# Fillers, two transposes, a cast and several memsets of a fused attention and mixture kernel change place, under a new order

## Chip, cores, metric

One core of a Trainium2 chip runs the whole program. The metric is the device time of one execution in microseconds: 364.89 us as the median of 3 runs before the change (364.28 to 365.04).

## Reference, cut to what matters

```python
def reference(q, k, v, phi, w1, w2, w_in, w_out):
    # attention: B=4, H=8, S=576, D=64; heads 0-3 a window of 32, heads 4-7 of 128 with every 4th key
    scores = where(mask, q @ k.T / 8, -1e9)
    attn = softmax(scores) @ v
    x = attn.transpose(0, 2, 1, 3).reshape(2304, 512)
    # soft mixture: 8 experts with 4 slots each
    logits = x @ phi                               # 2304 x 32
    d = softmax over the tokens (axis 0)           # dispatch
    slot_input = (d.T @ x).reshape(8, 4, 512)
    slot_out = relu(slot_input @ w1[e]) @ w2[e]    # each expert e
    c = softmax over the slots (axis 1)            # combine
    x = c @ slot_out.reshape(32, 512)
    # dense layer
    h = x @ w_in                                   # 2304 x 2048
    return (h * sigmoid(h)) @ w_out                # 2304 x 512
```

## The kernel before, in words

**Stages.** Attention runs over 16 pairs of heads, four pairs to a batch. For pair n, SyncE loads q, k and v (`lq`, `lk`, `lv`), POOL spreads q into two halves of a buffer (`qx`, `qy`; for pair 0 `qy0` is VectorE's, line 178), TensorE makes the scores (`S`), VectorE the row maxima (`rm`), ScalarE the exponentials (`ex`), POOL normalizes (`nm`), VectorE transposes (`pt`), TensorE multiplies by v (`pv`), ScalarE copies (`xe`), TensorE transposes (`T`, line 312) and makes the logits (`lt`), and ScalarE stores x (`te`, line 315).

After each batch b comes its part of the dispatch softmax over the tokens, kept as a running maximum and a running sum: `da` (VectorE, maximum), `dt` (TensorE, transpose), `dm` (VectorE, line 381), `db` (TensorE, broadcast of the maximum), `dq` and `dr` (POOL and TensorE, the same maximum by rows), `dsub` (VectorE, line 397), `dex` (ScalarE, line 461), `dc` (TensorE, 40 matmuls with x), `dw`, `dwe`, `dacc` (rescaling), `ds` (VectorE, line 467: the sum in `acc`). Behind the last batch's `ds3`, `sit` transposes acc (TensorE, line 505), `sipz` (POOL) and `sipy` (VectorE) clear the padded buffer `x_sip`, and `sie` (VectorE, line 518) spreads the slots into it. `hzz` (POOL, line 514) clears the 2112 columns that `hr0` and `hr1` later fill.

The combine softmax runs beside it for each batch: `caa`, `cab`, `cac`, `cad`, `cae`, then `caf` (VectorE: a cast at line 417 and a subtraction at 418 into `cc`), `cag` (POOL, line 422), and `cb` (TensorE transposes, line 434; `cbB.0` has three, `cbB.1` has two), copied by `cbs`.

The experts are 16 steps `L1.i` (w1) and 16 steps `L2.i` (w2), each reading one weight of 128 x 2048 f32 (1,024 KB), with `he`, `ht`, `hr` (copy, transpose, relu) after each half of L1. `soe`, `sotm`, `sote` bring the slots' outputs back. In the dense layer `aq` multiplies them by w_in (so that 32 slots, not 2304 tokens, go through w_in), `ah` and `al` split the result into a high and a low part, `ac` lines them up; `h` multiplies by the combine weights, `si`, `gh`, `gl` make silu in two parts, `om` multiplies by w_out (three matmuls a step), `oe` evacuates. w_in and w_out arrive as 64-bit words, and VectorE converts each piece in three steps (lines 630, 632, 634: `cva`, `cvb`, `cvi` for w_in, `cvc`, `cvd`, `cvo` for w_out); `wh` and `wl` split w_out.

**Order.** Every step is put into a list with `op(name, engine, cost, deps, fn)`. `list_schedule` deals them out by a cost model: at each moment an engine takes its ready step with the longest remaining path plus `PRIO` of its kind. Each engine then runs its steps in that order. SyncE's loads have a fixed order: ten at the start, then the letters of `ATT` (q: q and k of the next pair, v: the next v, w: the next w1 or w2 weight, i and o: the first w_in and w_out parts), then the rest. A load waits for its buffer: w2.8 to w2.15 go where w1.0 to w1.7 or later were and wait for `L1.1` to `L1.8`; `lwi0.0` waits for `L1.11`, `lwo0` for `L1.14`. All loads before w_in's second piece (`lwi1.0`) are the same set in both kernels.

**Fillers.** `fl` and `ff` are bf16 matmuls of 512 columns whose results nobody reads. They read `cc`, the combine softmax's buffer, and run on TensorE at the start (`FILL`: how many ahead of pairs 0 to 3) and in the last dispatch softmax (`TAIL`: after which step, how many). L1.0 waits for all `ff`.

## Time and profile before

| what | us |
|---|---|
| median of 3 runs (lowest, highest) | 364.89 (364.28, 365.04) |
| the profiled execution | 362.87 |
| its span, first to last instruction | 361.1 |
| TensorE busy | 348.3 (96%) |
| VectorE busy | 236.9 (66%) |
| ScalarE busy | 165.0 (46%) |
| POOL busy | 74.2 (21%) |
| transfers | 70.02 MB, 194 GB/s over the span |

All times of rows are microseconds from the span's first instruction. The profiled execution is one run; its span leaves out 1.77 us around it. PE is TensorE, PEld its weight loads, DVE VectorE, ACT ScalarE, SPq SyncE's transfer queue. All TensorE helpers go through line 86, so there a row is told from the next by what it reads.

### The profile page before, as it was taken

How to read it: one execution, taken by the hardware profiler on the slowest of the kernel's cores; microseconds unless marked ns; L12 is line 12 of the kernel's file. 1: busy time of each engine (PE TensorE's matmuls, PEld its weight loads, DVE VectorE, ACT ScalarE, POOL GpSimd, SP SyncE). 2: the span in 40 equal slices, each digit the busy share in tenths (PEclk: the TensorE clock that was granted, in tenths of full speed). 3: DMA queues.
4: the chain of work that ended last, by engine and by line, in shares of the span. 5: the costliest groups of instructions: out<-in, count | busy, mean ns of one | idle time of the engine just before them, and what ended most of it. 6: DMA issues, size and time to landing. Idle time of an engine off the chain costs nothing.

```text
span 361.1 us, 7977 instructions
## 1 busy us (share of the span) xinstructions
PE 348.3 (96%) x3121; PEld 263.7 (73%) x3121; DVE 236.9 (66%) x547; ACT 165.0 (46%) x558; POOL 74.2 (21%) x121
## 2 busy tenths in 40 slices
PE   7999999999699999999999999999999999999995
PEld 3577778787423346778888888878788888888884
DVE  5778767799611559999999964479444744474445
ACT  1699998896140126595444342255452222222220
POOL 6779798575410000000000000000000000000000
PEclk9999999999999999999999999999999999999999
DMA  7999999999989999371830000000000300030004
GB/s 263 408 401 409 401 405 382 409 415 416 420 328 416 393 422 420 123 298 33 343 108 8 2 0 1 2 0 3 0 0 2 145 29 2 1 145 31 0 0 174
DMA packets 17460, 70.02 MB, mean 194 GB/s; under 512 B 1936, under 2 KB 2448, under 8 KB 11664
## 3 DMA queue, kind: packets, MB, share of 16 engines
q1 hardware_dynamic: 17424, 69.53, 49.1%
q8 instruction: 24, 0.39, 0.4%
q14 instruction: 12, 0.10, 0.1%
HBM read 64.80 MB, written 4.72 MB: 193 GB/s over the span
## 4 chain that ended last, share of the span: by engine, by line
PE 87%; DVE 6%; ACT 4%; issue 1%; POOL 0%; DVEq 0%; ACTq 0%
PE ps L86 83%; PE ps L312 3%; ACT rt_px L232 1%; ACT rv_astk L711 1%; DVE stats L227 1%; PE ps L434 1%; DVE ra_wif L634 1%; DVE ra_wif L632 1%; DVE chi L417 0%; ACT rt_gtm L794 0%; ACT x_gz L799 0%; POOL rt_px L249 0%; DVE w_gy L804 0%; DVE cc L418 0%; DVE ra_a L178 0%
## 5 line engine op out<-in xcount | busy, mean ns | idle before, releaser
L86 PE MATMUL ps<-w_ws,x_gz 128*128 128x512 f32 x432 | 107.5, 392 | 0.0
L794 ACT ACTIVATE rt_gtm<-ps 128x384 f32<-128x384 f32 x96 | 46.6, 492 | 103.4 <-PE ps L86 102.9
L86 PEld LDWEIGHTS ps<-w_ws,x_gz 128*128 128x128 f32 x432 | 80.1, 188 | 16.6 <-issue 0.4
L86 PE MATMUL ps<-w_ws,w_gy 128*128 128x512 f32 (+1 forms) x219 | 53.7, 389 | 0.0
L232 ACT ACTIVATE rt_px<-ps,spaced 128x64 f32<-128x64 f32 x144 | 43.7, 332 | 11.6 <-DVE spaced L228 10.8
L86 PEld LDWEIGHTS ps<-w_ws,w_gy 128*128 128x128 f32 x219 | 40.4, 188 | 8.1
L801 DVE CAST x_gz<-rt_gtm 128x384 fp32r<-128x384 f32 x52 | 18.6, 358 | 41.4 <-ACT rt_gtm L794 41.3
L804 DVE TENSOR_TENSOR x_gz<-rt_gtm,x_gz 128x384 fp32r<-128x384 f32 x64 | 35.5, 557 | 4.2
L86 PE MATMUL ps<-ct_ct,rv_astk 128*128 128x384 f32 x96 | 32.0, 340 | 0.2 <-ACT rv_astk L711 0.2
L232 ACT ACTIVATION_READ_ACCUMULATOR rt_px<-ps,spaced 128x1 f32 x144 | 32.1, 223 | 0.0
L801 DVE CAST w_gy<-rt_gtm 128x384 fp32r<-128x384 f32 x28 | 10.0, 357 | 20.2 <-ACT rt_gtm L794 20.1
L86 PEld LDWEIGHTS ps<-ct_ct,rv_astk 128*128 128x128 f32 x96 | 17.9, 188 | 5.3 <-ACT rv_astk L711 1.0
L249 POOL TENSOR_TENSOR rt_px<-rt_px,stats 128x576 f32<-128x576 f32 (+2 forms) x17 | 18.9, 1115 | 6.7 <-DVE stats L245 2.8
L804 DVE TENSOR_TENSOR w_gy<-rt_gtm,w_gy 128x384 fp32r<-128x384 f32 x32 | 17.8, 557 | 2.7 <-ACT rt_gtm L794 0.4
L86 PE MATMUL ps<-rk_ws,x_gz 128*128 128x512 f32 x72 | 18.0, 394 | 0.4 <-ACT x_gz L799 0.4
L86 PE MATMUL ps<-rb_ws,x_gz 128*128 128x512 f32 x72 | 18.0, 393 | 0.0
L86 PEld LDWEIGHTS ps<-rk_ws,x_gz 128*128 128x128 f32 x72 | 13.3, 188 | 3.3 <-ACT x_gz L799 0.7
L86 PEld LDWEIGHTS ps<-rb_ws,x_gz 128*128 128x128 f32 x72 | 13.3, 188 | 2.8 <-DVE rb_ws L755 0.2
L227 DVE TENSOR_REDUCE stats<-ps 128x9 f32<-128x576 f32 x16 | 11.8, 736 | 5.3 <-PE ps L86 3.3
L86 PE MATMUL ps<-cc 128*128 128x512 bf16 x37 | 11.0, 433 | 4.0 <-DVE cc L418 2.3
L86 PEld LDWEIGHTS ps<-rb_a,rv_v 128*64 128x64 f32 x320 | 13.1, 137 | 2.1 <-issue 1.1
L86 PE MATMUL ps<-rb_a,rv_v 128*64 128x96 f32 (+2 forms) x320 | 14.6, 241 | 0.0
(224 smaller groups left out, 520.1 us busy)
## 6 DMA issues: line engine op xcount, KB each, us to landing
w_wi<-in_w_in SPq DMA_DIRECT2D x7, 1024.0 KB, 12.8
w_wo<-in_w_out SPq DMA_DIRECT2D x5, 1024.0 KB, 6.9
rk_k<-in_k SPq DMA_DIRECT2D x12, 288.0 KB, 8.0
rs_raw<-in_v SPq DMA_DIRECT2D x9, 288.0 KB, 7.6
rs_raw<-in_q SPq DMA_DIRECT2D x8, 288.0 KB, 8.9
w_more<-in_q SPq DMA_DIRECT2D x8, 288.0 KB, 9.3
...
```

The costliest lines, as they stand in the source:

```text
L86: pe.matmul(out, lhsT=lhsT, rhs=rhs, start=start, stop=stop, skip_group_check=True)
L227: dve.tensor_reduce(out=mxs[:, n % 2], in_=ps[:, c:c + 64 * NJ].rearrange("p (j c) -> p j c", c=64), axis=AXX, op=ALU.max)
L232: act.activation(out=preg(n)[:, j, :], in_=sj(n, j), func=ACTF.Exp, scale=D ** -0.5, bias=nmx[:, r, j // 3, j % 3:j % 3 + 1], accum_out=su ...
L249: pool.tensor_tensor(out=p, in0=p, in1=rinv[:, n % 2, j0:j1].rearrange("p (j o) -> p j o", o=1).to_broadcast([128, j1 - j0, 64]), op=ALU.mult)
L312: pe.transpose(ps[0:m, c:c + 128], x[:, 128 * t:128 * t + m], ident)
L434: pe.transpose(cbank(b, k)[:, c:c + m], cc[0:m, t].rearrange("p r s -> p (r s)"), ident[0:m, 0:m])
L632: dve.scalar_tensor_tensor(out=out, in0=hi, scalar=0xC0000000, in1=out, op0=ALU.bitwise_and, op1=ALU.bitwise_or)
L634: dve.scalar_tensor_tensor(out=out, in0=lo, scalar=29, in1=out, op0=ALU.logical_shift_right, op1=ALU.bitwise_or)
L711: act.copy(out=asl(f)[32 * r:32 * r + 32], in_=(aqh if r < 2 else aql)[rows])
L794: act.activation(out=gtm(u), in_=hb(u), func=ACTF.Silu)
L801: dve.tensor_copy(ghalf(u, 0), gtm(u))
L804: dve.tensor_tensor(out=ghalf(u, 1), in0=gtm(u), in1=ghalf(u, 0), op=ALU.subtract)
```

## The change

The filler groups become three: two matmuls behind `dt3` (in bank 0 instead of 3), two behind `dr3`, one behind `cb1.1`; `dr3` also waits for the first. `caf1` waits for `dsub3`, `caf2` for `sie`, `cb1.1` for `dc3`, `cb1.0` for `sit`, `hzz` for `sie`. Of the start's VectorE memsets, `ilb`, `izb1` and `it1` wait for `qy0`. The first filler block has 8 matmuls instead of 7. The cost model lets the four engines start at 0.75 us and gives the first fillers 0.42 us each. `ATT` and all of `PRIO` are new.

```diff
@@ -455,7 +455,7 @@
            lambda b=b: mm(mb[:, 128:160], ones[0:1].to_broadcast([1, 128]), dm[:, 0:NS], True, True))
         op(f"dq{b}", "POOL", .28, [f"dm{b}", f"dr{pb}" if b else None], lambda b=b: pool.tensor_copy(
             dm[:, NS:].rearrange("p (r s) -> p r s", r=4), dm[:, 0:NS].rearrange("p (o s) -> p o s", o=1).to_broadcast([1, 4, NS])))
-        op(f"dr{b}", "PE", .3, [f"dq{b}", f"dsub{b}" if b < B - 1 else exn(NPAIR - 2), f"dw{pb}" if b else "ix"],
+        op(f"dr{b}", "PE", .3, [f"dq{b}", "ff0" if b == B - 1 else None, f"dsub{b}" if b < B - 1 else exn(NPAIR - 2), f"dw{pb}" if b else "ix"],
            lambda b=b: mm(drb(b), dm[:, NS:], ones[0:1], True, True))
         op(f"dsub{b}", "DVE", .27, [f"db{b}", f"la{b}", f"dc{pb}" if b else None], lambda b=b: dsub(b))
         op(f"dex{b}", "ACT", .24, [f"dsub{b}"], lambda b=b: act.activation(out=le, in_=le, func=ACTF.Exp))
@@ -475,12 +475,12 @@
         op(f"cac{b}", "ACT", .24, [f"cab{b}"], lambda b=b: act.activation(out=cn, in_=cn, func=ACTF.Exp))
         op(f"cad{b}", "DVE", .66, [f"cac{b}", f"cae{pb}" if b else None], lambda b=b: ca4(b))
         op(f"cae{b}", "POOL", .42, [f"cad{b}"], lambda b=b: pool.tensor_tensor(out=cn, in0=cn, in1=bc5(csm), op=ALU.mult))
-        op(f"caf{b}", "DVE", .68, [f"cae{b}"] + ([f"cb{pb}.0", f"cb{pb}.1"] if b else []), lambda b=b: ca6(b))
+        op(f"caf{b}", "DVE", .68, [f"cae{b}", "sie" if b == 2 else "dsub3" if b == 1 else None] + ([f"cb{pb}.0", f"cb{pb}.1"] if b else []), lambda b=b: ca6(b))
         op(f"cag{b}", "POOL", 1.2, [f"caf{b}"], lambda b=b: ca7(b))
         for k in range(2):
             e = exn(NPAIR - 1)
             free = (((e,), (e,)), ((f"xe{NPAIR-1}",), (e,)), ((f"xe{NPAIR-1}", f"te{NPAIR-1}"), (f"la{B-1}", f"da{B-1}")), (("cbs1.0",), ("he1",)))[b][k]
-            op(f"cb{b}.{k}", "PE", (.45, .3)[k], [f"cag{b}", *free], lambda b=b, k=k: cb(b, k))
+            op(f"cb{b}.{k}", "PE", (.45, .3)[k], [f"cag{b}", {"1.1": "dc3", "1.0": "sit"}.get(f"{b}.{k}"), *free], lambda b=b, k=k: cb(b, k))
             op(f"cbs{b}.{k}", "ACT", (.37, .21)[k], [f"cb{b}.{k}", "cbs0.0" if b or k else "L1.0"], lambda b=b, k=k: cbe(b, k))
 
 
@@ -511,7 +511,7 @@
 
     op("sipz", "POOL", .63, ["dc3"], lambda: pool.memset(sip(0, 704), 0.0))
     op("sipy", "DVE", .39, ["dc3"], lambda: dve.memset(sip(704, 352), 0.0))
-    op("hzz", "POOL", 1.8, ["sipz"], lambda: pool.memset(reg("sip", 1056, 2112), 0.0))
+    op("hzz", "POOL", 1.8, ["sie"], lambda: pool.memset(reg("sip", 1056, 2112), 0.0))
 
     def sie():
         dst = sipad().rearrange("p (e x) -> p e x", x=132)[:, :, 0:128].rearrange("p e (g i) -> p e g i", i=32)[:, :, :, 0:4]
@@ -919,25 +919,25 @@
         for _ in range(c):
             mm(bank[b], fsrc[:, 0:128], fsrc[:, 0:512], True, True)
 
-    for k, (d, c) in enumerate(TAIL):
-        op(f"ff{k}", "PE", .225 * c, [d, f"te{NPAIR-1}"], lambda c=c: fill(c, 3))
+    for k, (d, c, b) in enumerate(TAIL):
+        op(f"ff{k}", "PE", .225 * c, [d, f"te{NPAIR-1}" if b else exn(NPAIR - 1)], lambda b=b, c=c: fill(c, b))
         ops["L1.0"][2].append(f"ff{k}")
 
     def ilb():
         dve.memset(lb[64:128, 128:160], -1e30)
         dve.memset(ps[64:128, TC + 512:TC + 640], 0.0)
 
-    op("ilb", "DVE", .2, [], ilb)
+    op("ilb", "DVE", .2, ["qy0"], ilb)
     op("ifl", "DVE", .3, [], lambda: dve.memset(cc.rearrange("p t r s -> p (t r s)")[:, 0:256], 1.0))
     op("pex", "ACT", 1.6, ["ifl"], lambda: act.activation(out=t4[:, 7:8], in_=cc[:, 0, 0, 0:1], func=ACTF.Exp))
     for n in FILL:
-        op(f"fl{n}", "PE", .225 * FILL[n], ["ifl", f"S{n-1}" if n else None], lambda n=n: fill(FILL[n]))
+        op(f"fl{n}", "PE", (.225 if n else .42) * FILL[n], ["ifl", f"S{n-1}" if n else None], lambda n=n: fill(FILL[n]))
     for n in range(2):
         op(f"iza{n}", "POOL", .57, [], lambda n=n: pool.memset(zq(n, 1), 0.0))
-        op(f"izb{n}", "DVE", .57, [], lambda n=n: dve.memset(zq(n, 0), 0.0))
+        op(f"izb{n}", "DVE", .57, ["qy0"] if n else [], lambda n=n: dve.memset(zq(n, 0), 0.0))
     op("izm", "POOL", 2.7 + 1.3 * VY.count("POOL"), ["iza1", "qx0"], izm)
     for n in range(2):
-        op(f"it{n}", "DVE", .85, [], lambda n=n: dve.memset(ptreg(n), 0.0))
+        op(f"it{n}", "DVE", .85, ["qy0"] if n else [], lambda n=n: dve.memset(ptreg(n), 0.0))
     op("ix", "POOL", .7, ["izm"], ix)
     op("cmask", "SP", 1.2, [], cmask)
     op("cip", "SP", .37, [], lambda: sp.dma_start(out=ip, in_=a["ip"]))
@@ -993,7 +993,7 @@
         fixed = {"xe": (4, 5), "T": (3, 4), "te": (3, 4), "lt": (6,), "la": (6,), "da": (6,), "ht": (2,), "hr": (2,), "soe": (3,),
                  "aqh": (6,), "aq": (6,), "ah": (6,), "al": (6,), "aqr": (7,), "ahr": (7,), "alr": (7,)}
         fixed.update(dict.fromkeys(("dt", "dm", "db", "dsub", "dc", "ds", "sit", "sie", "fl"), (7,)))
-        fixed["ff"] = (3,)
+        fixed["ff"] = (TAIL[i[0]][2],) if kind == "ff" else ()
         if kind == "pv":
             return {4 if i[1] == (2 if i[0] == NPAIR - 1 else 1) else 5}
         return {3} if n.startswith("L2") else set(fixed.get(kind, ()))
@@ -1031,19 +1031,19 @@
 OMS = 1
 LOOK = 0.2
 AHEAD = 3.0
-ATT = "vqqwvvwqqwvqwwvvqwqvwqqvwvqwqvwvvwqwqwwvvwwwwwwwwwwwwwwiwoiwwowiw"
+ATT = "qqvqwvwwqvqwvvwqvvqwqwvqvqwvvqwwvqwwwqvwwwvwwwwwwwwwwwwwwooiwwwii"
 URG = {"al", "ac", "ah", "sote", "aqh", "sotm", "soe", "on", "aqr", "ahr", "alr", "aq", "h", "gh", "gl", "si"}
 SAME = {"DVE": .04, "ACT": .04, "PE": .0, "POOL": .02}
 LAT = {"SP": 2.85, "POOL": .05, "PE": .18, "ACT": .12, "DVE": .12}
 MORE = {"ex": .04, "xe": .1, "te": .1, "vy": .07, "rm": .06, "rc": .08, "da": .06, "la": .06, "dsub": .05, "dw": .05, "nm": .04, "dex": .1, "dwe": .1, "pt": .02}
 LATE = ((0, 0), (10, .8), (25, 1.6), (110, 2.4))
 TICK = 10.24 / 3
-TAIL = (("te15", 2), ("db3", 3), ("dc3", 2), ("sit", 2))
-FILL = {0: 7, 1: 6, 2: 6, 3: 9}
+TAIL = (("dt3", 2, 0), ("dr3", 2, 3), ("cb1.1", 1, 3))
+FILL = {0: 8, 1: 6, 2: 6, 3: 9}
 QP = range(1, 16)
 VY = ("DVE", "ACT", "DVE", "ACT")
 DUTY = {"dc": .5, "dt": .5, "db": .2, "dr": .0, "sit": .5, "ht": .28, "sotm": .28}
-PRIO = {'T': 0, 'nm': -3.27, 'om': -1, 'cae': -20, 'dacc': -0.36, 'pre': -0.5, 'dw': 0.5, 'da': -3.66, 'dsub': 1.06, 'soe': -4, 'rc': -0.5, 'wh': 1.11, 'dr': 0, 'dex': 4.35, 'cbs': 3, 'te': -5.49, 'dc': 2, 'he': -2, 'ah': -2.36, 'L': -1, 'S': -19.48, 'sie': -6, 'si': 0.16, 'pv': -0.65, 'cvd': 1, 'pt': -0.73, 'wl': 10, 'iq': -1, 'cad': 1.61, 'L2a': 0.5, 'cvi': 10, 'ex': -2.53, 'cvo': -4.15, 'aqr': 7.13, 'db': 4, 'ahr': -10, 'it': 10, 'gl': 3.48, 'gh': 10.52, 'dt': 0, 'ds': 6.4, 'la': -6, 'ng': 0.5, 'cac': -20, 'ht': -6, 'sote': 0.14, 'izm': -4, 'hzz': 4, 'sipy': 1, 'sit': -2.69, 'aq': 4, 'caf': 9.01, 'sipz': -7.48, 'al': 0.5, 'vy': -10.26, 'oe': 4, 'ac': 0.5, 'vx': -0.22, 'fz': 6, 'cab': -0.5, 'sotm': 10, 'alr': 0.01, 'cb': 4, 'lt': 2, 'cvb': -2.91, 'hr': 7.4, 'caa': 6, 'xe': 6.74, 'dwe': -3.34, 'on': -1.21, 'qx': -3, 'rm': -5.98, 'izq': -6.69, 'dm': -4, 'crs': 21.31, 'h': -0.95, 'cva': 0.96, 'cvc': -2.39, 'qy': -5.01, 'ix': -20.55, 'cag': 0, 'dq': -2.51, 'aqh': -4.57, 'fl': -2.55, 'ifl': 10, 'pex': 9.83, 'izb': -18.79, 'iza': -0.33, 'M': -1, 'ilb': 6, 'ff': 2}
+PRIO = {'T': 1.39, 'nm': 2, 'om': -2.0, 'cae': -2, 'dacc': 20, 'pre': -0.39, 'dw': 0.11, 'da': 20.17, 'dsub': 19.03, 'soe': -20, 'rc': 20.4, 'wh': 6.69, 'dr': 3, 'dex': 0.29, 'cbs': 1.51, 'te': -5.11, 'dc': -4, 'he': 10, 'ah': -4, 'L': -1, 'S': -1.43, 'sie': 6, 'si': -4.76, 'pv': 0.74, 'cvd': -4, 'pt': 1.57, 'wl': -4, 'iq': 10, 'cad': -1, 'L2a': -6, 'cvi': 2.11, 'ex': -3.75, 'cvo': -5.92, 'aqr': -3.34, 'db': 3.22, 'ahr': 0, 'it': -18.87, 'gl': -4, 'gh': -4.9, 'dt': -1.73, 'ds': 1.26, 'la': -0.47, 'ng': 0.5, 'cac': 9.13, 'ht': -3, 'sote': 5.24, 'izm': 0.31, 'hzz': -5.08, 'sipy': 10, 'sit': -6.08, 'aq': 10.56, 'caf': -1.65, 'sipz': -1.57, 'al': -6.1, 'vy': -9.58, 'oe': 4, 'ac': -4, 'vx': 1, 'fz': -10.07, 'cab': 20, 'sotm': -1, 'alr': -3, 'cb': -0.5, 'lt': 0.55, 'cvb': -4.67, 'hr': 1, 'caa': -7.65, 'xe': 2, 'dwe': -0.5, 'on': -1.51, 'qx': -4.09, 'rm': -1.72, 'izq': -6.69, 'dm': -4, 'crs': 1, 'h': -1.95, 'cva': -0.5, 'cvc': -6.64, 'qy': -3.36, 'ix': -1.65, 'cag': 1.87, 'dq': 9.0, 'aqh': -20, 'fl': 0, 'ifl': -0.41, 'pex': 0.18, 'izb': -4, 'iza': 3, 'M': 1.54, 'ilb': 0.32, 'ff': 3.95}
 
 
 def list_schedule(ops):
@@ -1080,9 +1080,9 @@
     for n in reversed(topo):
         level[n] = ops[n][1] + max((level[s] + gap(n, s) for s in succ[n]), default=0.0)
     idx = {n: i for i, n in enumerate(ops)}
-    free, ready = {}, {}
+    free, ready = dict.fromkeys(("PE", "ACT", "DVE", "POOL"), .75), {}
     when = dict.fromkeys(ops, 0.0)
-    events = [(0.0, idx[n], n) for n in ops if need[n] == 0]
+    events = [(0.0, idx[n], n) for n in ops if need[n] == 0] + [(.75, -1, None)]
     heapq.heapify(events)
     order = []
     work = {}
```

## Rows read from the trace of the kernel before

**Rows 1.** The page: share of the DMA engines in 40 slices of the span, in tenths.

```profile
DMA  7999999999989999371830000000000300030004
```

**Rows 2.** The chain of waits: start, us, what.

```profile
157.68 199.55 PE ps L86 x945
```

**Rows 3.** Timeline of VectorE, 99 to 160: start, us, what, idle before and its releaser.

```profile
133.35 0.76 DVE L630 TENSOR_SCALAR w_wif<-w_wi 128x512 uint32<-128x512 uint32 x2 [0.28 <-DMA w_wi<-in_w_in]
...
151.18 0.69 DVE L634 SCALAR_TENSOR_TENSOR ra_wif<-w_wi,ra_wif 128x512 uint32<-128x512 uint32 x1
```

**Rows 4.** Stretch, length, busy PE PEld DVE ACT POOL, granted clock, DMA share, GB/s.

```profile
133.35:151.87 18.52, 18.08 (x161) 14.11 (x162) 17.08 (x35) 10.28 (x28) 0.00 (x0) 1.00 0.72 298
```

**Rows 5.** The same view, around the start of L1.

```profile
98.00:100.00 2.00, 0.85 (x6) 0.27 (x10) 1.42 (x4) 0.00 (x0) 0.58 (x2) 1.00 1.00 418
100.00:102.00 2.00, 2.00 (x24) 0.65 (x20) 0.00 (x0) 1.18 (x5) 0.69 (x2) 1.00 0.63 262
102.00:104.00 2.00, 2.00 (x24) 0.52 (x16) 0.68 (x3) 1.84 (x4) 0.46 (x1) 1.00 0.73 164
```

**Rows 6.** Timeline of SyncE, 99 to 160: the load of w2.8.

```profile
101.67 0.33 SPq L534 DMA_DIRECT2D w_w2.8_1693<-in_w  x1
```

**Rows 7.** Timeline of TensorE, 84 to 101.

```profile
92.27 0.59 PE L86 MATMUL ps<-cc 128*128 128x512 bf16 x2 [0.47 <-ACT x_xb L315]
92.79 0.40 PE L86 MATMUL ps<-hsb,ones 1*128 1x32 f32 x2
...
93.98 0.47 PE L434 MATMUL ps<-ip,cc 128*128 128x128 f32 x2
94.38 1.45 PE L86 MATMUL ps<-x_xb,le 128*32 128x129 f32 x40
...
96.20 0.49 PE L434 MATMUL ps<-ip,cc 128*128 128x128 f32 x3
96.53 0.27 PE L505 MATMUL ps<-ip,acc 128*128 128x128 f32 x1
99.15 0.61 PE L86 MATMUL ps<-cc 128*128 128x512 bf16 x2 [2.35 <-DVE cc L418]
99.69 1.06 PE L86 MATMUL ps<-ct_w1.0_243,x_sip 128*32 128x512 f32 x8
```

**Rows 8.** Timeline of VectorE, 84 to 101.

```profile
84.17 0.21 DVE L417 CAST chi<-cn 128x160 fp32r<-128x160 f32 x1
...
91.83 0.28 DVE L381 TENSOR_REDUCE hsb<-ps 1x32 f32<-1x128 f32 x1 [0.38 <-PE ps L86]
...
95.90 0.35 DVE L467 SCALAR_TENSOR_TENSOR acc<-ps,wgt,acc 128x129 f32<-128x129 f32 x1 [0.69 <-PE ps L86]
...
96.76 1.74 DVE L417 CAST chi<-cn 128x160 fp32r<-128x160 f32 x1
...
99.01 0.28 DVE L518 COPY x_sip<-ps 128x128 f32<-128x128 f32 x1
```

**Rows 9.** Timeline of POOL, 84 to 101: the large memset.

```profile
96.55 1.86 POOL L514 MEMSET x_sip<- 128x2112 f32 x1
```

**Rows 10.** Timeline of ScalarE, 84 to 101: the last dispatch exponential.

```profile
93.58 0.34 ACT L461 ACTIVATE le<-le 128x160 f32<-128x160 f32 x1 [0.34 <-DVE le L397]
```

**Rows 11.** Timeline of VectorE, 0 to 14: the spread of pair 0's q.

```profile
4.65 0.95 DVE L178 TENSOR_SCALAR ra_a<-rs_raw 64x576 f32<-64x576 f32 x1
```

**Rows 12.** Timeline of POOL, 0 to 14: its copy of the same load.

```profile
3.68 0.66 POOL L180 COPY ra_a<-rs_raw 64x576 f32<-64x576 f32 x1 [1.86 <-DMA rs_raw<-in_q]
```

**Rows 13.** Timeline of TensorE, 0 to 14: first fillers, S0, S1.

```profile
1.19 3.17 PE L86 MATMUL ps<-cc 128*128 128x512 bf16 x7 [1.19 <-DVE cc L931]
5.70 2.19 PE L86 MATMUL ps<-rk_k,ra_a 128*64 128x64 f32 x36 [1.35 <-DVE ra_a L178]
...
10.37 1.27 PE L86 MATMUL ps<-rk_k,rb_a 128*64 128x64 f32 x36
```

**Rows 14.** Busy time by engine, summed over 13.26 to 91.4 us.

```profile
sum 78.14, PE 76.41 PEld 60.05 DVE 62.33 ACT 66.16 POOL 59.77; mean PE 12.73 PEld 10.01 DVE 10.39 ACT 11.03 POOL 9.96
```

## Prediction

> **What bounds the kernel now.** I read three views in this order: the 40 slices of the page for the transfers, the chain of waits for the end, then the timelines of the stretches that the change touches.
>
> The slices [rows 1] show two regimes. The DMA row stands at 9 from the second slice to the sixteenth (9 to about 144 us), with one 8 in the twelfth slice (99 to 108 us); behind it the queue is nearly empty. The chain of waits [rows 2] ends in one piece of TensorE work without a gap, 945 matmuls from 157.68 to 357.24 us. So the time is the moment at which TensorE reaches 157.68 in a state from which it never waits again, plus a tail that the change leaves alone. Anything saved earlier counts only as far as it moves that moment.
>
> What sets it? On VectorE the w_in conversion that starts at 133.35 waits for its load [rows 3], the first 1,024 KB w_in piece behind the last w2 weights. From there to the conversion that ends at 151.87 (the input of aq3) VectorE is busy 17.08 of 18.52 us [rows 3, 4]. aq3, its low parts, their copies on ScalarE and the matmul at 157.68 follow. So the moment hangs on a landing, and the landing on how long the transfers sat idle. They did so once: at 418 GB/s before 100 us, then 262 and 164 GB/s in two stretches of 2 us [rows 5]. Lost: (418-262)x2 + (418-164)x2 = 820 KB, or 820/418 = 1.96 us. The reason is in SyncE's row: the load of w2.8 is issued at 101.67 [rows 6], because its buffer is the one that L1.1 has just read, and L1.0 starts only at 99.69 [rows 7].
>
> **Why L1.0 starts so late.** The last dispatch softmax is a serial ping-pong, and TensorE waits 2.35 us ahead of 99.15 [rows 7]. VectorE shows why [rows 8]: the spread copy sie, which L1 needs, stands at 99.01 behind caf2. That cast took 1.74 us from 96.76, where another of its shape took 0.21 us; POOL's 2112-column memset ran from 96.55 to 98.41 [rows 9], and the cast ended 0.09 us after it.
>
> **The change, part by part.**
>
> (a) Cast and large memset behind sie. The transpose sit ends at 96.80. The two small memsets that sie also needs stand ahead of the cast on VectorE and ahead of the large memset on POOL, so they are done by 96.76. So sie may run at 96.92 instead of 99.01: -2.09 us. Both now follow sie. Nothing on the path waits for the cast (its transposes are cb2, in the experts' second half) or the memset (hr0, behind the first half of L1), so I cost them at nothing; without that cover the cast costs up to 1.74-0.21 = 1.5 us.
>
> (b) Fillers. The two between te15 and db3 go: db3 runs at 92.79, while its input, the maximum at 91.83, is done at 92.11 [rows 7, 8]. The new ff0 sits in the wait for that maximum (two matmuls, 0.59 us, from about 91.8), so db3 may start at about 92.35: -0.45. The three behind db3 become two behind dr3 and still fit beside VectorE and ScalarE. The two just ahead of L1.0 (99.15 to 99.69) go; L1.0 then starts some 0.1 us after sie's end (99.29) instead of 0.4: -0.3.
>
> (c) Transposes cb1.1 and cb1.0. Today cb1.1 runs at 93.98, and dc3 starts at 94.38 though its exponential ended at 93.92 [rows 7, 10]: -0.33. Moved behind dc3, cb1.1 (0.47) and one filler (0.3) may hold sit back: without them it starts after ds3, 0.35 us at 95.90, so they have a hole of 0.45 us to lie in and cost 0 to 0.3. cb1.0 (0.49) now follows sit instead of preceding it and lies beside sie: -0.2 to 0. I take 0 for the pair. caf1 now waits for dsub3; VectorE has 0.69 us idle and more before ds3, so 0.7 us of caf1 fits if the low-urgency sums behind it yield; queued behind it are dw3 and the rescaling of acc, for which ds3 waits. Between 0 and +0.5; I take 0.
>
> Sum of (a) to (c): 2.09 + 0.45 + 0.3 + 0.33 = 3.2 us earlier for L1.0.
>
> (d) Start. qy0 starts at 4.65 behind memsets [rows 11], while POOL's copy of the same load starts at 3.68, when it lands [rows 12]. With it1, izb1 and ilb moved behind qy0, it can start at 3.68 and end at 4.63. The first filler block grows from 7 to 8; seven took 3.17 us from 1.19 [rows 13], so eight end at about 4.8, and S0 moves from 5.70 to 4.8: -0.9. S0 takes 2.19 us against 1.27 for S1's equal matmuls at 10.37; without the idle 1.35 us ahead of it it may shorten by up to 0.92, at worst not at all. I take 0, so -0.9 (bounds -1.8 and 0). The moved memsets land in VectorE's idle time behind qy0, while S0 runs.
>
> The Trainium skill bears on (a) and (d). SBUF — State Buffer, section "Who interferes with whom", says that VectorE's cast and plain tensor_scalar can share a port pair with GpSimd, and that whoever issues first holds it for the whole instruction. The 1.74 us cast agrees. By that rule qy0, released together with POOL's 0.66 us copy, may wait for it: (d) would be -0.3 instead of -0.9, rival 1 below would give 0.6 us more, and the forecast would stay, since it doesn't use the whole of (d). The row of qy0 (0.95 us, beside POOL memsets) suggests that such a wait is already in it.
>
> (e) New order. All priorities and the order of the loads change, so attention (13.3 to 91.4 us) is dealt anew. TensorE is busy 76.41 of 78.14 us there [rows 14]: at most 1.73 us to gain. A loss has no bound in a row; the longest single wait ahead of TensorE is the 2.35 us in rows 7, so I allow +2.4. Value: 0, since no row favours a sign. In the loads, two more w2 weights come ahead of w_in and w_out, whose first parts come in one group with the last w2. The bytes ahead of the 133.35 load are the same. SyncE now waits for L1.14 ahead of w2.14; w2.8 to w2.13, 6 x 1,024 KB or 15 us at 418 GB/s, lie ahead of that wait, more than the 13 us from L1.1 to L1.14, so the queue shouldn't run dry.
>
> **Sum.** L1.0 moves by -3.2 - 0.9 = -4.1 us, to about 95.6 (bounds 93 to 99). To close the transfer gap w2.8 must be issued 2 us earlier; -4.1 does it with 2.1 to spare. From there all loads land 1.96 us earlier, and no more, because the queue is then full throughout. VectorE starts the w_in conversions at 131.4 and the moment 157.68 becomes 155.7. The other 2.1 us turn into TensorE waiting for w2.14, w2.15 and aq's converted weights. So -2.0 us. The profiled execution of 362.87 us (span 361.1, 1.77 around it) would become 360.9; the median of the runs, 364.89, is 2.02 above that execution, and with the same difference the forecast is **362.9**. Its own range is 362.1 to 364.1 (gains of 0.8 to 2.8: L1.0 only 1 us earlier, or VectorE's 1.4 idle us partly used).
>
> **Rivals.**
>
> 1. The landing doesn't bind. If the new order keeps TensorE fed while the w_in conversions are late, the end moves by the whole 3.2 to 4.1: 360.8 to 361.7, about 361. For it: between 136.38 and 157.68 TensorE waits little, so matmuls might be shifted. Against it: 17.08 of 18.52 us of VectorE between landing and aq3. Chance 0.15.
>
> 2. Nothing comes through. Attention lasts over 2 us longer, so the transfer gap stays, or the saved 2 us are lost in the conversions: 364.9. Chance 0.15.
>
> 3. Slower: VectorE's order from the landing to aq3. There the low parts of the activations (gl), which TensorE needs next, compete with the conversions, and gl's priority falls from 3.48 to -4, wl's from 10 to -4, while cvb and cvc fall less. Each conversion step put ahead of a gl or wl on the path costs 0.69 us [rows 3]. It decides from the third such step on (2.0/0.69 = 2.9); five give +1.5: 366.4. For it: VectorE has no slack there. Against it: the conversions' priorities fall too, and a step ahead of gl isn't lost but done early. Chance 0.20.
>
> **Chances.** Forecast 0.50, rivals 0.15, 0.15 and 0.20. Measurement can tell about 0.2%, or 0.73 us, from no change. Faster: 0.50 + 0.15 = 0.65. Within: 0.15. Slower: 0.20. The range goes from 360.4 (rival 1 with part of S0's shortening) to 366.2 (short of rival 3's far half): about 0.13 is left out.
>
> **What would show it.** Right: sie directly behind sit, and L1.0 at 94 to 97.5; the cast still long but with nobody waiting; S0 near 4.8; transfers at 410 GB/s or more from 100 to 104; w2.8 issued before 100; the first w_in conversion that waits for its load near 131.4; the last gap of TensorE ending near 155.7. Wrong: L1.0 later than 97.7 (attention lost time), a gap in the transfers at another place, such as 105 to 115 behind SyncE's wait for L1.14, or a first aq that waits for the late w_in parts so long that TensorE's last gap moves less than the landing.

## The result, and the profile after

The changed kernel takes **359.85 us** (median of 4 runs, 359.53 to 360.57); four runs of the kernel before in the same comparison gave 364.58 (362.69 to 365.04). The ratio is 0.9883, 95% interval 0.9844 to 0.9921. A second measurement of both (e6_after below) gave 0.9892 [0.9857, 0.9927]. The forecast was 362.9 us and the range began at 360.4: the direction was right, but the gain of 4.7 us is more than twice the 2.0 that was forecast, and the time lies below the range.

The two profiled executions are much closer together: 362.87 us before and 360.57 us after, -2.30. So there are two things to find: what the 2.3 us are, and why the medians differ by twice as much.

The slices of the page (share of the DMA engines, in tenths) have no dip left at the twelfth slice, where [rows 1] has an 8; and in the chain of waits (start, us, what) TensorE's last piece without a wait begins at 154.78 instead of 157.68 [rows 2] (the chain splits it at 169.06 over 0.01 us):

```profile
DMA  7999999999999999462630000000000400040004
```

```profile
154.78 14.26 PE ps L86 x63
169.06 185.50 PE ps L86 x882
```

TensorE's timeline in the tail of the last dispatch softmax (start, us, instruction, idle time before and its releaser), against [rows 7]:

```profile
92.43 0.38 PE L86 MATMUL ps<-ip,gmx 128*1 128x128 f32 x2
92.75 0.60 PE L86 MATMUL ps<-cc 128*128 128x512 bf16 x2
93.28 0.40 PE L86 MATMUL ps<-hsb,ones 1*128 1x32 f32 x2
...
94.46 1.45 PE L86 MATMUL ps<-x_xb,le 128*32 128x129 f32 x40
95.84 0.53 PE L434 MATMUL ps<-ip,cc 128*128 128x128 f32 x2
96.31 0.39 PE L86 MATMUL ps<-cc 128*128 128x512 bf16 x1
96.64 0.33 PE L505 MATMUL ps<-ip,acc 128*128 128x128 f32 x1
96.81 0.49 PE L434 MATMUL ps<-ip,cc 128*128 128x128 f32 x3
97.42 1.06 PE L86 MATMUL ps<-ct_w1.0_283,x_sip 128*32 128x512 f32 x8
```

The 2.35 us wait is gone. L1.0 starts at 97.42 instead of 99.69, and everything from dt3 (92.43) to L1.0 takes 4.99 us. In the kernel before dt3 stood at

```profile
91.42 0.38 PE L86 MATMUL ps<-ip,gmx 128*1 128x128 f32 x2
```

so the same stretch took 8.27 us. VectorE shows why (same columns, the changed kernel), with POOL's large memset in the second fence:

```profile
97.08 0.29 DVE L518 COPY x_sip<-ps 128x128 f32<-128x128 f32 x1
...
97.92 1.07 DVE L413 TENSOR_SCALAR csm<-csm 128x5 f32<-128x5 f32 x1
...
99.85 0.24 DVE L417 CAST chi<-cn 128x160 fp32r<-128x160 f32 x1 [0.44 <-POOL cn L477]
```

```profile
97.11 1.86 POOL L514 MEMSET x_sip<- 128x2112 f32 x1
```

sie (L518) now stands 0.11 us behind sit's end. The memset now meets another VectorE instruction, the 128x5 one of L413, and it is that one that ends 0.02 us behind the memset. The cast, ahead of sie before, comes 2.8 us after it and takes 0.24 us.

The start (TensorE, VectorE, POOL, same columns), the load of w2.8, and the w_in conversion that waited for its load before, with VectorE's step ahead of it, against [rows 13], [rows 11], [rows 12], [rows 6] and [rows 3]:

```profile
4.82 1.27 PE L86 MATMUL ps<-rk_k,ra_a 128*64 128x64 f32 x36 [0.22 <-POOL zm L901]
...
9.02 1.27 PE L86 MATMUL ps<-rk_k,rb_a 128*64 128x64 f32 x36 [0.61 <-POOL rb_a L180]
```

```profile
3.79 0.46 DVE L178 TENSOR_SCALAR ra_a<-rs_raw 64x576 f32<-64x576 f32 x1 [0.95 <-DMA rs_raw<-in_q]
```

```profile
3.82 0.95 POOL L180 COPY ra_a<-rs_raw 64x576 f32<-64x576 f32 x1 [2.00 <-DMA rs_raw<-in_q]
```

```profile
99.41 0.33 SPq L534 DMA_DIRECT2D w_w2.8_1683<-in_w  x1
```

```profile
130.61 0.43 DVE L634 SCALAR_TENSOR_TENSOR w_wif<-w_wi,w_wif 128x256 uint32<-128x256 uint32 x1
131.14 0.77 DVE L630 TENSOR_SCALAR w_wif<-w_wi 128x512 uint32<-128x512 uint32 x2
```

The transfers around the start of L1 (stretch, length, busy times of the engines, granted clock, DMA share, GB/s), against [rows 5]:

```profile
98.00:100.00 2.00, 2.00 (x24) 0.53 (x18) 1.53 (x4) 1.31 (x4) 1.42 (x2) 1.00 1.00 418
100.00:102.00 2.00, 2.00 (x24) 0.65 (x20) 0.77 (x3) 0.54 (x2) 1.19 (x2) 1.00 0.91 332
102.00:104.00 2.00, 2.00 (x24) 0.63 (x20) 0.50 (x3) 1.29 (x2) 0.45 (x1) 1.00 1.04 426
```

Of the 1.96 us of lost transfer time (418-332)x2/418 = 0.41 us are left. The conversion starts at 131.14 instead of 133.35, -2.21. It no longer waits: VectorE's step ahead of it ends at 131.04, so the row tells only that the load had landed by then.

Two more places on TensorE decide between the explanations below. The expert step L2.8 waited 0.38 us for `hr1` (line 548) before, and doesn't wait now (first fence: before, then after). The first `aq`, 64 matmuls, stands behind L2.15 and the slots' outputs (second fence, the same two kernels):

```profile
123.82 1.07 PE L86 MATMUL ps<-w_w2.8_1693,x_sip 128*32 128x512 f32 x8 [0.38 <-DVE x_sip L548]
120.99 1.06 PE L86 MATMUL ps<-w_w2.8_1683,x_sip 128*32 128x512 f32 x8
```

```profile
133.47 1.95 PE L86 MATMUL ps<-w_wif,lg 128*32 128x128 f32 x64
130.64 1.95 PE L86 MATMUL ps<-w_wif,lg 128*32 128x128 f32 x64
```

The times of the kernel before are best understood with the mean granted clock of each execution beside them. In the comparisons below it ran 76 times: 49 executions had a mean of 0.997 or more (median 362.69 us, 361.80 to 364.58), 27 had 0.993 to 0.995 (median 364.65, 363.56 to 365.21); the median of all 76 is 363.14. What spreads the 49 over 2.8 us isn't shown. All ten executions of the changed kernel had 0.998 or more (median 360.2).

### The profile page after: what moved, and what is told of

The parts are those of the page before. It is cut to its first block, busy times and chain, and to the rows that moved or that the text cites. A ratio compares the mean times of both kernels' runs of the same rounds, so it can differ in the third digit from the quotient of the medians.

```text
span 358.4 us, 7976 instructions
## 1 busy us (share of the span) xinstructions
PE 346.7 (97%) x3118; PEld 263.2 (73%) x3118; DVE 236.9 (66%) x547; ACT 165.1 (46%) x558; POOL 74.5 (21%) x121
## 4 chain that ended last, share of the span: by engine, by line
PE 90%; ACT 3%; DVE 2%; POOL 1%; issue 1%; DMA 1%; DVEq 0%; ACTq 0%; POOLq 0%
PE ps L86 86%; PE ps L312 3%; ACT rt_px L232 1%; DMA rs_raw<-in_q 1%; PE ps L434 1%; POOL rv_v L907 1%; ACT rv_astk L711 1%; ACT rt_px L301 1%; ACT rt_gtm L794 0%; POOL rb_a L180 0%; ACT x_gz L799 0%; POOL ra_a L180 0%; DVE stats L227 0%; ACT x_xb L315 0%; DVE spaced L244 0%
## 5 line engine op out<-in xcount | busy, mean ns | idle before, releaser
L86 PEld LDWEIGHTS ps<-ra_a,rv_v 128*64 128x64 f32 x320 | 13.3, 137 | 3.2 <-issue 1.4
L86 PE MATMUL ps<-ra_a,rv_v 128*64 128x96 f32 (+2 forms) x320 | 15.1, 241 | 0.6 <-issue 0.3
```

Of the source, the lines that this page charges most:

```text
L86: pe.matmul(out, lhsT=lhsT, rhs=rhs, start=start, stop=stop, skip_group_check=True)
```

## The experiments

In all of them "the tail" is the stretch from dt3 to L1.0. "L2.15" is how long the last w2 step takes (about 1.06 us without a wait). "Conversion" stands for the start of the w_in conversion that in the kernel before waits for its load; its wait for that load stands in brackets. "First aq" is the start of the 64 matmuls shown above, and "last gap" the start of TensorE's last piece without a wait (in e8_mix the start of the same step). This table gives the marks of each profiled execution, in us, and the comparison of all runs.

| kernel | L1.0 | w2.8 issued | L2.15 | conversion (wait) | first aq | last gap | first aq to gap | this execution | median (n) | ratio, 95% |
|---|---|---|---|---|---|---|---|---|---|---|
| before | 99.69 | 101.67 | 1.06 | 133.35 (0.28) | 133.47 | 157.68 | 24.21 | 362.87 |  |  |
| after | 97.42 | 99.41 | 1.04 | 131.14 (none) | 130.64 | 154.78 | 24.14 | 360.57 | 359.85 (4) | 0.9883 [0.9844, 0.9921] |
| e0_before | 99.20 | 101.19 | 1.47 | 133.32 (0.73) | 133.38 | 157.57 | 24.19 | 362.75 | 362.89 (12) | 0.9983 [0.996, 1.0005] |
| e1_start | 99.20 | 101.18 | 1.85 | 133.69 (1.10) | 133.75 | 157.99 | 24.24 | 363.14 | 363.46 (12) | 0.9986 [0.9962, 1.0009] |
| e2_tail | 96.81 | 98.80 | 1.55 | 130.99 (0.79) | 131.07 | 155.28 | 24.21 | 360.43 | 360.78 (7) | 0.9922 [0.9893, 0.9951] |
| e3_both | 95.35 | 97.34 | 2.98 | 131.16 (2.06) | 131.23 | 155.41 | 24.18 | 360.65 | 360.69 (6) | 0.9908 [0.988, 0.9935] |
| e4_bridge | 98.37 | 100.36 | 1.07 | 131.87 (none) | 132.16 | 156.33 | 24.17 | 361.50 | 362.11 (12) | 0.9959 [0.9935, 0.9983] |
| e5_nofill | 99.19 | 102.80 | 1.69 | 135.14 (0.95) | 135.21 | 159.41 | 24.20 | 364.66 | 363.07 (12) | 0.9985 [0.9958, 1.0011] |
| e6_after | 97.33 | 99.32 | 1.92 | 132.65 (1.05) | 131.41 | 156.09 | 24.68 | 361.78 | 360.29 (6) | 0.9892 [0.9857, 0.9927] |
| e7_short | 95.03 | 97.01 | 1.06 | 129.62 (0.80) | 129.06 | 153.25 | 24.19 | 358.43 | 358.69 (6) | 0.9848 [0.9816, 0.9881] |
| e8_mix | 95.45 | 97.44 | 2.21 | 131.10 (1.07) | 129.82 | 154.87 | 25.05 | 365.60 | 366.16 (6) | 1.0088 [1.0056, 1.012] |
| e9_hzz | 97.46 | 99.45 | 1.36 | 131.47 (0.62) | 131.53 | 155.72 | 24.19 | 360.93 | 361.47 (12) | 0.9953 [0.9936, 0.9971] |
| e10_before | 100.40 | 103.52 | 1.53 | 135.70 (0.80) | 135.76 | 159.95 | 24.19 | 365.16 | (1) |  |
| e11_start | 98.54 | 101.46 | 1.62 | 133.72 (0.88) | 133.78 | 157.99 | 24.21 | 363.15 | (1) |  |

### e0_before, e1_start, e2_tail, e3_both: the start and the tail, each alone and together

e0_before is the kernel before, unchanged. e1_start takes the start alone: one filler more ahead of S0, and VectorE's order there (the names are those of the kernel).

```diff
-VectorE: ifl it0 it1 iq0 iq1 iq2 iq3 ilb iq4 izb0 izb1 qy0
+VectorE: iq0 ifl iq1 iq2 izb0 iq3 iq4 it0 qy0 izb1 ilb it1
-fl0: 7 fillers
+fl0: 8 fillers
```

e2_tail takes the tail alone, with the order of the changed kernel on four engines; e3_both has both edits. Everything else, the order in attention and in the conversions too, is that of the kernel before.

```diff
-TensorE: dt3 ff0 db3 dr3 ff1 cb1.1 dc3 ff2 cb1.0 sit ff3 L1.0
+TensorE: dt3 ff0 db3 dr3 ff1 dc3 cb1.1 ff2 sit cb1.0 L1.0
-POOL: cag1 dq3 cab2 cae2 sipz hzz cag2 cab3
+POOL: dq3 cag1 sipz cab2 hzz cae2 cag2 cab3
-VectorE: ... ds3 sipy fz caf2 sie caa3 ...
+VectorE: ... caf1 dacc3 sipy ds3 fz sie cad2 caa3 caf2 ...
```

> The kernel before, unchanged, so that its own executions can be laid side by side. If executions of one program agree, every span lies within 0.3% (1.1 us) of 361.1 and the new trace has its steps where the first one had them: S0 at 5.70 for 2.19 us, L1.0 at 99.69, the last gap of TensorE ending at 157.68. If the first trace was a fast one among slower ones, the median is 363 to 365 and the new trace shows in which stretch 1 to 2 us are lost.

> The kernel before with the start alone: it1, izb1 and ilb behind qy0, 8 fillers instead of 7; order of everything else and all loads as before. S0 near 4.8. Landing theory (the end follows the landing of the w_in piece, which moves by no more than L1.0 does and no more than 2.0 us): L1.0 0.9 to 1.8 us earlier and the end 0.9 to 1.8 us earlier. TensorE theory (the end follows L1.0 all the way): the same 0.9 to 1.8 us. New-order theory (the start is absorbed in attention and the gain of the change comes from its priorities): 0 to 0.3 us.

> The kernel before with the tail alone: fillers, cb1.0, cb1.1, caf1, caf2 and hzz where the changed kernel has them, start, attention and loads as before. Both theories: L1.0 about 3.2 us earlier. Landing theory: the end 1.6 to 2.2 us earlier, because the loads had only 2.0 us of idle time to give back. TensorE theory: 3.0 to 3.4 us earlier. New-order theory: under 1 us.

> The kernel before with start and tail as in the changed kernel, but its own priorities and load order. L1.0 4.1 to 5 us earlier. Landing theory: the end no more than 2.2 us earlier, as in the tail alone. TensorE theory: 4.1 to 5 us earlier. New-order theory: clearly less than the changed kernel's 4.3 us, and the rest is the order's.

Measured: e0_before's twelve executions run from 362.16 to 364.58, two of them with the lower clock. In its profiled one L1.0 is 0.49 us earlier than in the first profile and the last gap only 0.11, because L2.15 takes 1.47 us instead of 1.06.

The start alone is no measurable gain (0.9986, interval across 1), where 0.9 to 1.8 us were expected if it comes through. S0 starts at 4.75 and S1 at 8.94 instead of 10.31, but in this execution the lead of 1.4 us shrinks through the pairs of attention and L1.0 starts at 99.20, as in e0_before. The tail alone gives 0.9922, most of the whole. With both, L1.0 starts 1.46 us earlier than with the tail alone, and the end gains nothing: 360.69 against 360.78. Against the full-clock executions of the kernel before in this comparison (median 362.69) each of the two gains 2.0 us, inside the 1.6 to 2.2 expected if the transfers bind; if TensorE's own work did, e3_both would have gained 4.1 to 5. The reason is in e3_both's timelines of TensorE and VectorE and in its transfers:

```profile
128.70 1.05 PE L86 MATMUL ps<-w_w2.15_1826,x_sip 128*32 128x512 f32 x4 [0.88 <-DMA w_w2.15_1826<-in_w]
```

```profile
131.16 0.76 DVE L630 TENSOR_SCALAR w_wif<-w_wi 128x512 uint32<-128x512 uint32 x2 [2.06 <-DMA w_wi<-in_w_in]
132.68 0.29 DVE L707 TENSOR_TENSOR rv_astk<-ps,rv_astk 64x128 fp32r<-64x128 f32 x1 [0.76 <-ACT rv_astk L704]
```

```profile
98.00:100.00 2.00, 2.00 (x24) 0.60 (x20) 0.77 (x3) 0.60 (x2) 1.19 (x2) 1.00 1.02 426
100.00:102.00 2.00, 2.00 (x24) 0.65 (x20) 0.43 (x3) 1.22 (x2) 0.46 (x1) 1.00 1.02 418
```

No transfer time is lost any more, and two steps wait for loads: L2.15 on TensorE for the second half of w2.15, and VectorE 2.06 us for the w_in piece, the load right behind it. VectorE's wait costs nothing, because its next step (L707) waits 0.76 us more for ScalarE's copy of the first aq's product, and the first aq stands behind L2.15. The chain of waits goes the same way: from the load of w2.15 at 117.29 to L2.15, and on through TensorE. So from L1.0 at about 97 on the transfers bind, as the prediction said, and rival 1 falls here (rival 2, nothing comes through, falls with e2_tail); but the load that binds is not the one that the prediction named.

### e4_bridge and e9_hzz: the 2.35 us wait alone

e4_bridge keeps every order of the kernel before and replaces the two fillers ahead of L1.0, which wait for the cast's product, by nine that read the mask, which is there from the start, so TensorE is busy through the wait. e9_hzz moves one instruction: POOL's large memset, behind the copy cag2.

```diff
-ff3: 2 fillers, operand cc
+ff3: 9 fillers, operand maskid
```

```diff
-POOL: sipz hzz cag2 cab3
+POOL: sipz cag2 hzz cab3
```

> The kernel before in its own order; only the two fillers ahead of L1.0 are replaced by nine that read the mask buffer instead of cc and so don't wait for caf2: they fill TensorE's 2.35 us wait behind sit. L1.0 doesn't come earlier (0 to 0.5 us). Clock theory (executions of the kernel before differ because the granted clock falls in some of them around that wait): the executions with a mean granted clock of 0.993 to 0.995 vanish, the spread of 361.9 to 365.1 shrinks to under 1.2 us, and the median falls from 363.5 to 362.2 to 362.8. Landing theory alone: no change of the median (within 0.4 us) and the same spread.

> The kernel before in its own order; only the 2112-column memset is put behind cag2 in POOL's queue, so that it no longer runs beside caf2's cast. If the memset held the cast back, the cast takes 0.2 to 0.3 us instead of 1.74 and L1.0 comes 1.3 to 1.6 us earlier; landing theory: the end 1.0 to 1.6 us earlier in executions at the full clock, and clock theory: TensorE's wait of 2.35 us shrinks to 0.8 to 1.0, so executions at 0.993 to 0.995 vanish and the median falls by 1.8 to 2.6 us. If the cast is slow for another reason, nothing changes.

Measured: e4_bridge 0.9959, e9_hzz 0.9953, and in both all 12 executions have a mean granted clock of 0.998 or more. In e9_hzz VectorE and TensorE read:

```profile
96.05 0.22 DVE L417 CAST chi<-cn 128x160 fp32r<-128x160 f32 x1
...
96.79 0.28 DVE L518 COPY x_sip<-ps 128x128 f32<-128x128 f32 x1
```

```profile
96.93 0.60 PE L86 MATMUL ps<-cc 128*128 128x512 bf16 x2 [0.84 <-DVE cc L418]
97.46 1.07 PE L86 MATMUL ps<-ct_w1.0_243,x_sip 128*32 128x512 f32 x8
```

The same cast in the same place takes 0.22 us once the memset isn't beside it (1.74 in [rows 8]). That one move brings sie to 96.79, cuts the wait from 2.35 to 0.84 us and carries 1.85 us to the last gap (155.72, against 157.57 in e0_before).

Both also show how much is the clock. Against the full-clock executions of the kernel before in the same comparisons (medians 362.38 and 362.61) e4_bridge gains 0.3 us and e9_hzz 1.1; the rest of the 1.5 us that each gains on the median is the lower group, which no longer occurs. For e9_hzz 1.8 to 2.6 us had been expected. e4_bridge doesn't part clock and order cleanly: its L1.0 came 0.83 us earlier than in e0_before, where 0 to 0.5 was expected.

### e5_nofill, e10_before, e11_start: where the clock falls

e5_nofill is the kernel before without the nine fillers of the tail. e10_before and e11_start are e0_before and e1_start once more, each for a single execution.

```diff
-ff0 ff1 ff2 ff3: 2, 3, 2, 2 fillers
+ff0 ff1 ff2 ff3: none
```

> The kernel before in its own order without the nine fillers of the last dispatch softmax. Clock theory: the mean granted clock is at or below 0.995 in every or nearly every execution, and the time is 364 to 366, at or above the slow half of the kernel before; its trace shows the stretch of the lower clock. Landing theory alone: L1.0 0.3 to 0.7 us earlier and the end the same or 0.5 us earlier.

> The kernel before again, for a look at an execution with a lower mean clock: of 76 executions of it 27 had a mean granted clock of 0.995 or less (median 364.65 us, 363.56 to 365.21) and 49 had 0.997 or more (median 362.69, 361.80 to 364.58). Theory: TensorE's clock falls behind its 2.35 us wait ahead of L1.0. If this execution has 0.995 or less, the granted clock is then under 1.0 only between 96 and 106 us, w2.8 is issued at 102.4 to 103.2 instead of 101.2, the last gap ends at 158.7 to 160, and the time is 363.6 to 365.2. Rival: it falls elsewhere (the idle time ahead of S0, or the solid piece behind 157 us); then the lower stretch stands there, and w2.8 is issued within 0.3 of 101.2. If the mean is 0.997 or more (about 6 in 10), no stretch is under 1.0 and the run tells nothing.

> The kernel of e1_start again (the new start, the old tail with its 2.3 us wait), for the same look: 7 of its 12 executions had a mean granted clock of 0.993 to 0.995 (363.44 to 364.24 us), 5 had 0.998 or more (361.65 to 363.14). Theory: if this one has 0.995 or less, the clock is under 1.0 only between 96 and 106 us, w2.8 is issued 1.2 to 2 us later than 101.2, the last gap ends at 158.7 to 160, time 363.4 to 364.3. Rival: the lower stretch stands elsewhere and w2.8 is within 0.3 of 101.2. With 0.998 or more nothing is told.

Measured: 11 of 12 executions of e5_nofill have a mean clock of 0.989 to 0.995, and both single executions have 0.994 and 0.993. e10_before shows the place, by the same columns as above:

```profile
96.00:98.00 2.00, 1.09 (x11) 0.61 (x6) 1.75 (x5) 0.00 (x0) 1.79 (x2) 1.00 1.03 430
98.00:100.00 2.00, 0.57 (x2) 0.13 (x2) 1.70 (x4) 0.00 (x0) 0.69 (x1) 0.83 0.99 414
100.00:102.00 2.00, 2.00 (x10) 0.40 (x12) 0.00 (x0) 0.00 (x0) 0.86 (x2) 0.50 0.79 328
102.00:104.00 2.00, 2.00 (x20) 0.56 (x16) 0.03 (x1) 1.58 (x6) 0.00 (x0) 0.82 0.17 70
104.00:106.00 2.00, 2.00 (x24) 0.60 (x20) 0.65 (x3) 1.44 (x2) 0.45 (x1) 1.00 0.69 176
```

and TensorE there, in e10_before and then in e0_before, the same program at full clock:

```profile
99.43 1.03 PE L86 MATMUL ps<-cc 128*128 128x512 bf16 x2 [2.35 <-DVE cc L418]
100.40 1.94 PE L86 MATMUL ps<-ct_w1.0_243,x_sip 128*32 128x512 f32 x8
102.11 1.34 PE L86 MATMUL ps<-w_w1.1_314,x_sip 128*32 128x512 f32 x8
```

```profile
98.67 0.61 PE L86 MATMUL ps<-cc 128*128 128x512 bf16 x2 [2.35 <-DVE cc L418]
99.20 1.07 PE L86 MATMUL ps<-ct_w1.0_243,x_sip 128*32 128x512 f32 x8
100.09 1.04 PE L86 MATMUL ps<-w_w1.1_314,x_sip 128*32 128x512 f32 x8
```

TensorE idles 2.35 us, and what follows runs at a granted clock of 0.50, the 1.2 GHz level: the two fillers take 1.03 instead of 0.61, L1.0 1.94 instead of 1.07. The load of w2.8 waits for L1.1, so it is issued 103.52 - 99.43 = 4.09 us after the fillers' start, against 101.19 - 98.67 = 2.52. The transfers, which idle just then, lose the difference (70 GB/s from 102 to 104), and the last gap stands 159.95 - 99.43 = 60.52 us behind the fillers' start instead of 58.90. So one fall of the clock costs 1.6 us, and no other stretch of this execution is below 1.00. e11_start has the same picture two microseconds earlier (0.76, 0.50 and 0.89 from 96 to 102), and e5_nofill again (0.77, 0.50 and 0.88 from 98 to 104, behind a wait of 2.69 us). Its times missed what was expected, though: 364 to 366 was expected, and the median is 363.07. Its one execution at full clock is the fastest (361.24, against a median of 363.35 of the others), so without the fillers the kernel seems faster apart from the clock; one execution can't show it.

Against that: two of seven executions of e2_tail and three of six of e8_mix show a mean of 0.993 to 0.995 too, though no wait of more than 0.5 us is left in their tails. Their profiled executions aren't among them, so where it fell there isn't known. The wait is the usual occasion, not shown to be the only one.

e11_start tells one more thing: here the early start did reach L1.0 (98.54 against 100.40 at the same low clock in e10_before), while e1_start lost it on the way. Why attention sometimes keeps the lead and sometimes not isn't settled.

### e6_after: the changed kernel again

> The changed kernel, unchanged, beside the others on one chip. Landing theory plus clock theory: 359.6 to 360.6, spread under 1.2 us, mean clock 0.998 or more in each execution; against the median of the kernel before -3.0 to -3.8 us, of which 2.2 to 2.7 from the landing and the conversions' order and the rest from the lower clock that no longer occurs.

Measured: 360.29 us; five executions from 359.99 to 360.54, and the profiled one, 361.78, the slowest. It has L1.0 and the issue of w2.8 within 0.1 us of the first profile, at full clock, yet here the conversion does wait for its load, and starts 1.5 us later:

```profile
132.65 0.79 DVE L630 TENSOR_SCALAR w_wif<-w_wi 128x512 uint32<-128x512 uint32 x2 [1.05 <-DMA w_wi<-in_w_in]
```

L2.15 takes 1.92 us instead of 1.04. SyncE shows that the difference arises in the queue: the three w_in loads that it issues from 116 us on take 5.51 us to issue instead of 4.09. What held them isn't shown; it means that a single profile of this kernel carries 1.2 us of chance (361.78 against 360.57).

### e7_short: do the transfers set the end?

e3_both without the load of the last 512 KB of w2.

```diff
-op("lw2b", "SP", 1.23, d, lambda: load_w2(15, 2, 4))
+op("lw2b", "POOL", 1.23, d, lambda: pool.memset(tiles["w2.15"][:, 1024:2048], 0.0))
```

> Start and tail in the order of the kernel before (as e3_both), with the last 512 KB of w2 not loaded but cleared by POOL: all w_in and w_out pieces behind it land 1.2 us earlier; half of one expert's second layer is left out of the result. Landing theory: the conversion that waited for its load at 131.16 starts 1.0 to 1.3 us earlier and the end is 1.0 to 1.3 us earlier than e3_both's 360.69. TensorE theory (its own work bounds it once L1.0 is early): the end moves by under 0.3 us.

Measured: 358.69 against 360.69 for e3_both, 2.0 us less, where 1.0 to 1.3 were expected and 512 KB at 418 GB/s are 1.25 us. The first aq moves by 2.17 us and the last gap by 2.16, the conversion only by 1.54. So it is the first aq that the end follows. The edit takes away the very load for which L2.15 waited, beside making the queue shorter; the two can't be told apart here, but either way it is a load that held TensorE in e3_both.

### e8_mix: the new order behind L1.0 alone

e3_both up to L1.0, and from there the order of all engines and of the loads of the changed kernel.

```diff
-ATT = "...wwwwwwwwiwoiwwowiw"
+ATT = "...wwwwwwwwwwooiwwwii"
```

> Up to L1.0 the order of e3_both (start and tail moved, attention as in the kernel before, L1.0 near 95.3), from there on the changed kernel's order of every engine and of the loads. Landing theory: the conversion behind the landing starts at 131 to 132 as in e3_both and in the changed kernel, and because the changed kernel's order of the conversions takes 23.5 us from there to TensorE's last gap instead of 24.3, the end is 0.5 to 1.0 us earlier than e3_both's 360.69: 359.7 to 360.2, no better than the changed kernel's 360.3 by more than 0.6. TensorE theory: L1.0 2 us earlier than in the changed kernel, so 358.3 to 359.

Measured: slower, 1.0088, where 0.5 to 1.0 us less than e3_both was expected. The last gap stands at 154.87 instead of 155.41, with the conversion at the same moment (131.10 and 131.16). This isn't a gain of the conversions' order: in e3_both the first aq, held by L2.15, set the gap, while here it is at 129.82 already and the conversion's load sets it (a wait of 1.07 us, and no further wait behind it). But the piece that was solid in every other kernel breaks up. The waits of TensorE from 154 us on, as a total, their number and the longest:

```profile
PE ps L86 <- ACT rt_gtm L794: 2.8, 4, 0.9
```

```profile
227.76 1.08 PE L86 MATMUL ps<-w_wif,lg 128*32 128x128 f32 x32 [0.58 <-ACT rt_gtm L794]
```

TensorE's order there is that of the changed kernel, where the same matmul starts 0.26 us behind its predecessor; here it waits for an activation that reads the same accumulators. I read it as a buffer shared in another rotation, because the order ahead of it differs; that reading is argued, not shown. So the run shows that orders cut from two kernels don't simply add.

## Why the prediction was right and wrong

**What bounds the kernel: the transfers, but not through the conversion that was named.** In all eleven profiled executions with the old order behind L1.0, the last gap stands 24.17 to 24.24 us behind the first aq, in e7_short too; its distance from the w_in conversion runs from 23.63 to 24.46. In ten of them VectorE's step behind that conversion waits another 0.74 to 0.97 us for ScalarE, behind the first aq (0.80 in the kernel before). So the wait of 0.28 us at 133.35, on which the prediction hung the end, lay off the path. The first aq follows L2.15, which reads the second half of w2.15, the load just ahead of that w_in piece. In the profiled execution of the kernel before no matmul waits for a load between L1.0 and the last gap: TensorE waits 1.3 us there, for ScalarE and VectorE. In e3_both L2.15 does wait for its load. So the ceiling of about 2 us on the gain holds (e2_tail and e3_both), one load earlier in the queue than the prediction put it.

**(a) to (c), the tail: right.** Forecast -3.2, measured 8.27 us (91.42 to 99.69) before and 4.99 after, -3.28. The parts: sie 0.11 us behind sit instead of 2.21 (forecast -2.09, measured -2.1); dt3 to db3 0.85 us instead of 1.37 (forecast -0.45); L1.0 0.05 us behind sie's end instead of 0.40 (forecast -0.3); and dc3, at 94.46, 0.04 us behind the end of its exponential instead of 0.46 (forecast -0.33). One detail was wrong and cost nothing: the cast wasn't long any more. The memset isn't held back by sie at all in time (it starts 0.03 us behind sie's start); it now meets L413. The Trainium skill, SBUF — State Buffer, section "Who interferes with whom", says that VectorE's cast and tensor_scalar can need the port pair that is shared with GpSimd, and that whichever engine issues second waits for the other's whole instruction. The rows agree three times: 1.74 us beside the memset, 0.22 in e9_hzz without it, and now 1.07 us for 128x5 elements, ended 0.02 us after it.

**(d) The start: right at its place, partly by luck, and not at L1.0.** S0 starts at 4.82 (forecast 4.8) and takes 1.27 us, the good end of its bound, so S1 is 1.35 us earlier. The moment comes from another cause than forecast: the eight fillers end at 4.61, and S0 waits 0.22 us more for POOL, whose copy, released with VectorE's qy0, took 0.95 us from 3.82 instead of 0.66. VectorE's qy0 took 0.46 us; the wait that the prediction feared for it seems to have fallen on POOL. Then dt3 stands at 92.43, 1.0 us later than before. Attention gave back about 2.4 us, which was the upper bound of (e), where I had taken 0. e3_both, with the same start and the old order in attention, has dt3 at 90.37, and e6_after, the changed kernel again, at 92.35; so the loss seems to belong to the new order, as far as so few executions can say. L1.0 comes at 97.42 instead of the forecast 95.6, still early enough for most of the transfer gap.

**(e) The new order behind L1.0: mis-sized by 0.6 us.** Here I took 0 as well. From L1.0 to the first aq it is 33.22 us after the change and 33.78 before. Of these 0.56 us, 0.38 are the wait of L2.8 for hr1, which is gone: hr1 stood on VectorE at 123.48, behind the combine's subtraction and a w_out conversion, and now stands at 120.42, ahead of both. From the first aq to the last gap it is 24.14 us, against 24.17 to 24.24, so the new order among the conversions, of which rival 3 expected a loss, neither gains nor loses there.

**The landing: not to be seen in the first profile, and the agreement of the profiled times is partly luck.** The forecast let 2.0 of 4.1 us through, held by the queue. In the changed kernel's first profile nothing on the path waits for a load, and TensorE carries all that L1.0 gained: 2.27 us to L1.0, 0.56 to the first aq and 0.07 to the last gap are 2.90 (157.68 to 154.78). That is rival 1's mechanism, with a smaller gain of L1.0 than it counted on. In e6_after the load does bind, and its conversion is only 0.70 us earlier than before (132.65). So the changed kernel stands where the two limits meet. The last piece is 0.22 us longer, and the span shrinks from 361.1 to 358.4. The time shrinks by only 2.30, since 2.17 us now lie around the span instead of 1.77; why isn't shown. The result, 360.57, is near the 360.9 that was forecast for this execution, but from other terms.

**The step that failed is the last one: "the median of the runs, 364.89, is 2.02 above that execution, and with the same difference the forecast is 362.9".** I carried the difference over as a constant; in the changed kernel the median lies 0.72 us below the profiled execution (359.85 and 360.57). That is 2.7 of the 3.05 us by which the forecast was off. The difference belonged to the very wait that the change removes. The profiled execution ran at full clock, while about a third of the executions (27 of 76) don't: the clock falls behind the 2.35 us wait, L1.0 and part of L1.1 run at half speed, the issue of w2.8 slips, and the end with it, by 1.6 us in e10_before's rows and by 2.0 between the medians of the two groups. The three times shown ahead of the prediction, 364.28 to 365.04, lie where the lower group lies (of the other 49 only one is above 364.28); their clocks aren't listed. In the changed kernel no execution of ten is of that group, so its median sits at its profiled execution, not 2 us above it. Against full-clock executions the gain is 362.69 - 360.2 = 2.5 us, near the 2.0 of the sum; the rest of the 4.7 is the lower group. How large that rest came out is also the luck of a small sample: three of the four executions that the changed kernel was compared with took 364.28 us or more. Against the median of all 76, 363.14, the gain is 3.0 us.
